# Token rows of k, b and y's scale made by TensorE from channel rows, with a third buffer of channel rows

## The chip, the cores and the metric

The kernel runs on one core of a Trainium2 chip. The metric is the device time of one launch in microseconds (us). Three runs of the kernel before gave 715.59, 718.26 and 719.21 us, a median of 718.26 us. The profiled execution took 721.54 us.

## The reference

Two stages follow one another. The first is a linear recurrence with a 40 x 40 state for each of 4 batches and 8 heads (32 sequences) over 768 steps; the second is a layer norm and a two-layer network on rows of 320 numbers (8 heads x 40).

```
for t in range(S):
    y[:, :, t] = einsum('bhd,bhde->bhe', rt, state)
    Sa = einsum('bhde,bhe->bhd', state, at)
    state = state * wt - Sa x bt + vt x kt
...
xn = (x - mean) / sqrt(var + 1e-06) * g_ln
out = x + maximum(xn @ w_ch1, 0.0) @ w_ch2
```

Everything is fp32. The weights arrive as float64 words and are turned to fp32 pairs in the kernel.

## The kernel before, in words

**Chunks.** The 768 steps are cut into 24 chunks of 32 steps. Within a chunk the recurrence becomes matrix products and a triangular solve, and only the 40 x 40 state passes from chunk to chunk. Running products of the decays w (a scan) scale a, b, k and y so that this works.

**prep(c)** (L137) works on *channel rows*: the tile `et` has 104 partitions (two halves of 40 channels at partitions 0 and 64), and holds w, a, and b and k of 16 sequences each. VectorE scans w forward (gE, L145) and backward (qE, L149), multiplies a by qE into `aT` (L156) and b, k in place by gE (L161); from chunk 6 on GpSimd does the two products. ScalarE copies aT into the block-diagonal `abd` (L160), TensorE multiplies b, k with abd (L174), VectorE applies a sign mask (`gk`, L179), and SyncE's queue writes gk and aT to device memory (d_g L186, d_a L190). `et` has two buffers, so that load_e(c+2) (L135) waits for the matmuls L174 of chunk c.

**load_cl(c)** (L306) does part of it a second time on *token rows* (128 partitions of batch and step): the tile `clt` brings w, k and b in that layout (L309). VectorE checks w (`wild`, L311), scans it both ways (L317, L321, with the reciprocal L320), and transposes both scans in 32 x 32 blocks (L325, L327; the second, `pi`, is y's scale). GpSimd multiplies k and b by the first (eight instructions, L335) into `xk[c % 2]`, and ScalarE copies that into its second half (L340).

**invert / invert2** (L193, L222) invert the triangular matrices of a slab of 2 or 4 chunks on VectorE (L204/L207, L237/L241). **chain(c)** (L361) is the step from state to state: right-hand sides (L368), solve (L348 to L358, or L264 to L275 for the first three slabs), new state (L380, then L386 on VectorE). **state(c)** and **post(c)** (L391, L405) make y: transposes (L397, L412), products (L425, masked in L431), and y (L439) from `xk`, scaled by `pi` into `xt` (L443).

**The network.** moe(g) (L589) handles two chunks. After norm (L553) there are ten blocks f, each with 8 matmuls into `ps_1` (L611), a relu on ScalarE (`hh`, L614), its remainder on VectorE (`hl`, L615), and 6 matmuls that add into two `ps_2` tiles `po` (L597). The result leaves through `ot` (L630). The six buffers of `xt` are freed by that last step.

**Order.** The opening (L661 to L703) is in hand-set order for VectorE and ScalarE; everywhere else a scheduler places instructions on each engine by priority and by its estimate of when an operand is ready. `BOOST` and `NUDGE` (L40, L41) shift priorities: preps have 2000 in their favour, load_cl -300. In L740, 90 groups of two filler matmuls (`warm`, L217) get the lowest priority of all. Each group takes one of the two `ps_2` buffers, and these are handed out in program order: the tiles `po` of the first moe come behind all 90. All DMAs of the loop go through SyncE's one queue, in order.

Of the kernel before, what the change touches and what calls it, by code (L numbers as in the profile page):

```python
# [11 lines left out]
F32 = mybir.dt.float32  # L12
# [22 lines left out]
AHEAD = 4  # L35
EARLY = 6
# [3 lines left out]
BOOST = dict(cg=-300, wg=-600, iv=-600, og=300, pg=2000)  # L40
# [5 lines left out]
def body(ctx, tc, et_in, cl_in, vr, rd, vt, w1, w1x_in, w2, gl, fe, fd, out):  # L46
# [30 lines left out]
    wild = const.tile([128, 10, C], U32, name="wild")  # L77

    et = [stat.tile([128, 2065], F32, name=f"et{i}") for i in range(2)]
# [6 lines left out]
    abd = stat.tile([128, 16, 2, C], F32, name="abd")  # L86
# [9 lines left out]
    def masks():  # L96
        for t, fills in ((sign, (-1.0, 1.0)), (mask, (1.0, 1.0))):
# [25 lines left out]

    d_g = [dr.tile([2, C, 32 * len(s), C], F32, name=f"d_g{i}") for i, s in enumerate(SLABS)]
# [3 lines left out]
    def load_e(c):  # L128
        if c < AHEAD:
            for r0 in HROW:  # L130
                sync.dma_start(out=et[c % 2][r0:r0 + D], in_=et_in[c, r0:r0 + D])
                if c == r0 == 0:
                    sync.dma_start(out=et[0][D:64], in_=et_in[0, D:64])
        else:
            sync.dma_start(out=et[c % 2][0:104], in_=et_in[c])  # L135

    def prep(c):  # L137

        t = et[c % 2]
        n = 528  # L140
        g = pre.tile([128, 16, 33], F32, name="gE")
        q = pre.tile([128, 16, 33], F32, name="qE")
# [8 lines left out]
            initial=0.0, op0=ALU.mult, op1=ALU.max)  # L151
        aT = pre.tile([128, 528], F32, name="aT", bufs=2)
# [5 lines left out]
        for hf in range(2):  # L158
            rs = slice(HROW[hf], HROW[hf] + D)
            nc.scalar.copy(out=abd[rs, :, hf], in_=aT[rs, 0:512].rearrange("p (h t) -> p h t", t=C))  # L160
# [9 lines left out]
        pg = pool_.tile([128, 2, 8, C], F32, name=name)  # L170
        for h in range(8):
            for bb in range(2):
                p = 8 * bb + h
                nc.tensor.matmul(  # L174
                    pg[64 * bb:64 * bb + 64, :, h], lhsT=t[R, 1041 + 64 * p:1105 + 64 * p],
                    rhs=abd[R, p], start=True, stop=True)
# [3 lines left out]
            out=gk, in0=pg.rearrange("p x h t -> p (x h) t"),  # L180
# [3 lines left out]
        for bb in range(2):  # L184
            m = 16 * (2 * k + bb)
            sync.dma_start(  # L186
                out=d_g[si][:, :, m:m + 16].rearrange("x a n t -> (x a) (n t)"),
# [784 lines left out]
```

## Time and profile before

| | before |
|---|---|
| median of 3 runs | 718.26 us |
| profiled execution | 721.54 us, of which 719.7 us are the span from the first to the last instruction |
| TensorE busy (matmul) | 594.4 us, 83% |
| VectorE busy | 579.7 us, 81% |
| ScalarE busy | 327.6 us, 46% |
| GpSimd busy | 287.1 us, 40% |
| mean granted TensorE clock | 0.885 |

Busy time of TensorE includes 73.4 us of filler matmuls (L217). The views read below are the table of groups (for each line: count, busy time, mean duration), the table by stretches of time (busy time of each engine, granted clock, share of the DMA engines), the waits, and single rows of the timeline.

### The profile page before, as it was taken

How to read it: one execution, taken by the hardware profiler on the slowest of the kernel's cores; microseconds unless marked ns; L12 is line 12 of the kernel's file. 1: busy time of each engine (PE TensorE's matmuls, PEld its weight loads, DVE VectorE, ACT ScalarE, POOL GpSimd, SP SyncE). 2: the span in 40 equal slices, each digit the busy share in tenths (PEclk: the TensorE clock that was granted, in tenths of full speed). 3: DMA queues.
4: the chain of work that ended last, by engine and by line, in shares of the span. 5: the costliest groups of instructions: out<-in, count | busy, mean ns of one | idle time of the engine just before them, and what ended most of it. 6: DMA issues, size and time to landing. Idle time of an engine off the chain costs nothing.

```text
span 719.7 us, 24705 instructions
## 1 busy us (share of the span) xinstructions
PE 594.4 (83%) x10386; PEld 525.3 (73%) x10386; DVE 579.7 (81%) x1290; ACT 327.6 (46%) x816; POOL 287.1 (40%) x328
## 2 busy tenths in 40 slices
PE   2786778877668878898878898888989888999995
PEld 2775667766557767787777777777868777889995
DVE  6888797999879949899859999969996989764631
ACT  3324666453333535344354445445536355656221
POOL 8514388456442416254415515623333213333000
PEclk9998878888798979797989988998999999999998
DMA  7787966556562557544567644776346434420100
GB/s 176 193 213 212 291 157 156 150 121 149 125 164 86 127 143 166 126 114 115 110 162 145 144 119 119 146 177 137 97 106 117 108 86 108 105 65 16 41 20 22
DMA packets 155380, 92.35 MB, mean 128 GB/s; under 512 B 126152, under 2 KB 136136, under 8 KB 152840
## 3 DMA queue, kind: packets, MB, share of 16 engines
q1 hardware_dynamic: 155264, 90.72, 52.1%
q8 instruction: 83, 1.36, 0.8%
q14 instruction: 33, 0.27, 0.1%
HBM read 72.06 MB, written 18.64 MB: 126 GB/s over the span
## 4 chain that ended last, share of the span: by engine, by line
DVE 38%; PE 27%; DMA 21%; ACT 6%; issue 5%; SPq 3%; POOL 0%; DVEq 0%; ACTq 0%
DMA et<-in_et_dram 11%; PE ps L611 9%; PE ps L597 8%; DVE yinv L207 5%; DVE ytmp L204 5%; DVE qE L149 3%; DMA r<-in_w_dram 3%; DVE gE L145 3%; DVE x L386 3%; DVE x5s L431 3%; DVE hl L615 2%; DMA d_tt<-yinv 2%; ACT x L358 2%; PE ps L217 2%; PE ps_a L412 1%
## 5 line engine op out<-in xcount | busy, mean ns | idle before, releaser
L611 PE MATMUL ps<-xh,w 128*128 128x256 f32 x480 | 123.5, 315 | 0.9 <-DVE xl L585 0.5
L597 PE MATMUL ps<-w,hh 128*128 128x320 f32 x480 | 118.7, 343 | 3.7 <-DVE ot L630 1.8
L614 ACT ACTIVATE hh<-ps 128x256 fp32r<-128x256 f32 x120 | 45.5, 382 | 129.8 <-PE ps L611 126.1
L611 PEld LDWEIGHTS ps<-xh,w 128*128 128x128 f32 x480 | 92.4, 211 | 5.9 <-issue 2.3
L597 PE MATMUL ps<-w,hl 128*128 128x320 f32 x240 | 77.4, 348 | 18.5 <-DVE hl L615 18.5
L597 PEld LDWEIGHTS ps<-w,hh 128*128 128x128 f32 x480 | 83.1, 206 | 7.8 <-ACT hh L614 2.3
L615 DVE SCALAR_TENSOR_TENSOR hl<-ps,hh 128x256 fp32r<-128x256 f32 x120 | 49.5, 415 | 45.5 <-ACT hh L614 43.0
L161 POOL TENSOR_TENSOR et<-et,gE 104x1024 f32<-104x1024 f32 x18 | 40.4, 2246 | 100.1 <-DVE gE L145 81.7
L217 PE MATMUL ps<-start,ident 128*128 128x160 f32 x360 | 73.4, 362 | 0.0
L611 PE MATMUL ps<-xl,w 128*128 128x256 f32 x240 | 73.3, 305 | 0.0
L204 DVE TENSOR_TENSOR ytmp<-yinv 128x30 f32<-128x30 f32 (+19 forms) x150 | 63.7, 425 | 6.6 <-DMA yinv<-d_g 4.7
L207 DVE TENSOR_TENSOR yinv<-yinv,ytmp 128x30 f32<-128x30 f32 (+19 forms) x150 | 64.4, 429 | 2.2
L217 PEld LDWEIGHTS ps<-start,ident 128*128 128x128 f32 x360 | 63.4, 233 | 2.3
L597 PEld LDWEIGHTS ps<-w,hl 128*128 128x128 f32 x240 | 47.6, 209 | 22.5 <-DVE hl L615 21.5
L145 DVE TENSOR_TENSOR_SCAN gE<-et,start 104x528 f32<-104x528 f32 x24 | 32.3, 1348 | 27.9 <-DMA et<-in_et_dram 27.7
L611 PEld LDWEIGHTS ps<-xl,w 128*128 128x128 f32 x240 | 50.9, 212 | 0.5 <-issue 0.3
L380 PE MATMUL ps_c<-x,xk 104*40 104x40 f32 (+1 forms) x1472 | 45.8, 212 | 3.6 <-ACT x L275 3.0
L160 ACT COPY abd<-aT 40x512 f32<-40x512 f32 x48 | 29.5, 615 | 41.7 <-DVE aT L156 19.1
L439 PE MATMUL ps_a<-xk,x5s 128*32 128x40 f32 (+1 forms) x1536 | 31.9, 213 | 19.0 <-DVE x5s L431 18.8
L386 DVE TENSOR_TENSOR x<-ps_c,x2s 40x320 f32<-40x320 f32 x92 | 44.8, 487 | 2.0
L380 PEld LDWEIGHTS ps_c<-x,xk 104*40 104x40 f32 (+1 forms) x1472 | 37.8, 125 | 11.3 <-ACT x L275 4.3
L358 ACT COPY x<-ps_c 32x160 f32<-32x160 f32 x144 | 40.7, 283 | 9.1 <-PE ps_c L353 6.0
(173 smaller groups left out, 1356.7 us busy)
## 6 DMA issues: line engine op xcount, KB each, us to landing
et<-in_et_dram SPq DMA_DIRECT2D x20, 838.9 KB
clt<-in_cl_dram SPq DMA_DIRECT2D x24, 485.5 KB
d_g<-gk SPq DMA_DIRECT2D x48, 128.0 KB
x<-in_vt_dram SPq DMA_DIRECT2D x48, 128.0 KB
d_a<-aT SPq DMA_DIRECT2D x24, 214.5 KB
vu<-in_vr_dram SPq DMA_DIRECT2D x24, 208.0 KB
x2s<-d_a SPq DMA_DIRECT2D x48, 82.5 KB
x5s<-in_rd_dram SPq DMA_DIRECT2D x48, 80.0 KB
```

Source lines behind the costliest of these rows:

```text
L145: nc.vector.tensor_tensor_scan(out=flat(g[R]), data0=t[R, 0:n], data1=flat(start0[R]), initial=0.0, op0=ALU.mult, op1=ALU.max)
L161: (nc.gpsimd if c >= EARLY else nc.vector).tensor_tensor(out=kb, in0=kb, in1=g[R, :, 0:C].unsqueeze(2).broadcast_to([104, 16, 2, C]), op=A ...
L204: nc.vector.tensor_tensor(out=tv, in0=y[0:n, j + 1:, j:j + 1].broadcast_to([n, m, j]), in1=y[0:n, j:j + 1, 0:j].broadcast_to([n, m, j]), o ...
L207: final["inv", si] = nc.vector.tensor_tensor(out=y[0:n, j + 1:, 0:j], in0=y[0:n, j + 1:, 0:j], in1=tv, op=ALU.add)
L217: nc.tensor.matmul(pw[:, 0:w], lhsT=ident, rhs=start0.rearrange("p h t -> p (h t)")[:, 0:w], start=True, stop=True)
L358: nc.scalar.copy(out=dst[:, :, :, j, 0:D], in_=pu[32 * j:32 * j + 32, :, :, hf])
L380: nc.tensor.matmul(pst[r0:r0 + D, h], lhsT=XK[FROW[hf], 1, hf, p], rhs=X2[FROW[hf], hf, p, 0:D], start=True, stop=True)
L386: nc.vector.tensor_tensor(out=X2n[r0:r0 + D, hf, ps, 0:D], in0=pst[r0:r0 + D], in1=pc.unsqueeze(2).broadcast_to([D, 8, D]), op=ALU.mult)
L597: nc.tensor.matmul(po[u], lhsT=l[:, us], rhs=ws[f"w2_{f}"][:, x], start=f == 0 and n == 0, stop=f == 9 and n == 2)
L611: nc.tensor.matmul(ph, lhsT=l, rhs=r, start=n == 0, stop=n == 7)
L614: nc.scalar.activation(out=hh, in_=ph, func=AF.Relu)
L615: nc.vector.scalar_tensor_tensor(out=hl, in0=ph, scalar=0.0, in1=hh.bitcast(F32), op0=ALU.max, op1=ALU.subtract)
```

## The change

load_cl is gone, and with it the tensor `cl`. The check of w (`wild`) moves into prep on channel rows (16 x 32 columns in place of 10 x 32). A new generator tokens(c) turns the scaled k, b in `et` and the scan qE to token rows: 64 matmuls with the identity matrix into three PSUM tiles, three ScalarE copies into `kt`, and one DMA of kt to a buffer `d_kb` in device memory. load_kb(c) replaces load_cl's end: two DMAs bring k, b into both halves of `xk[c % 2]` (so that GpSimd's products and ScalarE's copies go), and a third brings `pi`. `abd` goes as well: the products L174 become 32 matmuls on halves of 40 rows instead of 16 on 104, and read aT itself. `et` has three buffers (gE and qE two). Since the two halves of d_g change places, sign and indices follow. tokens(c) gets priority 0 ("tg"), load_cl's -300 is dropped; every other number stays.

```diff
-BOOST = dict(cg=-300, wg=-600, iv=-600, og=300, pg=2000)
+BOOST = dict(wg=-600, iv=-600, og=300, pg=2000)
...
-    et = [stat.tile([128, 2065], F32, name=f"et{i}") for i in range(2)]
+    et = [stat.tile([128, 2065], F32, name=f"et{i}") for i in range(ET)]
...
-        for hf in range(2):
-            rs = slice(HROW[hf], HROW[hf] + D)
-            nc.scalar.copy(out=abd[rs, :, hf], in_=aT[rs, 0:512].rearrange("p (h t) -> p h t", t=C))
...
-        for h in range(8):
-            for bb in range(2):
-                p = 8 * bb + h
+        for p in range(16):
+            for hf in range(2):
+                rs = slice(HROW[hf], HROW[hf] + D)
                 nc.tensor.matmul(
-                    pg[64 * bb:64 * bb + 64, :, h], lhsT=t[R, 1041 + 64 * p:1105 + 64 * p],
-                    rhs=abd[R, p], start=True, stop=True)
+                    pg[64 * hf:64 * hf + 64, p], lhsT=t[rs, 1041 + 64 * p:1105 + 64 * p],
+                    rhs=aT[rs, 32 * p:32 * p + 32], start=True, stop=True)
...
+    def tokens(c):
+        t, q = et[c % ET], qs_at[c]
+        pool_, name = (ps_1, "ps_1") if c <= AHEAD else (ps_a, "ps_a")
+        kt = pre.tile([128, 24, D], F32, name="kt")
+        for bb in range(2):
+            px = pool_.tile([128, 8, D], F32, name=name)
+            for h in range(8):
+                for hf in range(2):
+                    p, rs = 8 * bb + h, slice(HROW[hf], HROW[hf] + D)
+                    nc.tensor.matmul(
+                        px[ZROW[hf]:ZROW[hf] + 64, h], lhsT=t[rs, 1041 + 64 * p:1105 + 64 * p],
+                        rhs=ident[rs, rs], start=True, stop=True)
+            nc.scalar.copy(out=kt[:, 8 * bb:8 * bb + 8], in_=px)
+            yield
+        px = pool_.tile([128, 8, D], F32, name=name)
+        for h in range(8):
+            for b in range(4):
+                rs = slice(HROW[b // 2], HROW[b // 2] + D)
+                nc.tensor.matmul(
+                    px[32 * b:32 * b + 32, h], lhsT=q[rs, 8 * (b % 2) + h, 1:33],
+                    rhs=ident[rs, rs], start=True, stop=True)
+        nc.scalar.copy(out=kt[:, 16:24], in_=px)
+        sync.dma_start(out=d_kb[c], in_=kt)
+        yield
...
-    def load_cl(c):
...
+    def load_kb(c):
+        for hf in range(2):
+            rs = slice(ZROW[hf], ZROW[hf] + 64)
+            sync.dma_start(
+                out=xk[c % 2][rs, :, hf].rearrange("p x n e -> p x (n e)"),
+                in_=d_kb[c][rs, 0:16].rearrange("p n e -> p (n e)").unsqueeze(1).broadcast_to([64, 2, 16 * D]))
+        cls[c] = jit.tile([128, 8, D], F32, name="pi", bufs=3)
+        sync.dma_start(out=cls[c], in_=d_kb[c][:, 16:24])
```

The scheduler places nearly everything anew. Three places matter below. The first is TensorE's row where the network's second product (L597, in the changed kernel L601) first appears. Before, it stands in the solve of chunk 3 (L264), between the last filler groups (L217):

```order
L611 MATMUL ps_2737<-xl,w1x 128x256
L412 MATMUL ps_a<-ident,x_1_94 104x32 x8
L217 MATMUL ps_1374<-start_88,ident 128x160 x2
L217 MATMUL ps_1377<-start_88,ident 128x160
L264 MATMUL ps_c<-hbd,tt 32x40 x32
L597 MATMUL ps_2647<-w_0_2208,hh 128x320 x2
L597 MATMUL ps_2647<-w_0_2208,hl 128x320
L597 MATMUL ps_2647<-w_1_2330,hh 128x320 x2
```

In the changed kernel (filler L248, first product L615) the last two filler groups and the first rows of that product read:

```order
L248 MATMUL ps_1872<-start_88,ident 128x160 x2
L248 MATMUL ps_1875<-start_88,ident 128x160 x2
L601 MATMUL ps_3464<-w_0_3010,hh 128x320 x2
L601 MATMUL ps_3464<-w_0_3010,hl 128x320
L601 MATMUL ps_3464<-w_1_3147,hh 128x320 x2
L601 MATMUL ps_3464<-w_1_3147,hl 128x320
```

Counted along TensorE's rows, this place has moved back from the solve of chunk 3 to behind the solve of chunk 10. When chunk 10's right-hand sides are done, 30 blocks of the network's first product stand ahead of them before, 4 in the changed kernel; when chunk 11's are done, 35 in both. At the end of chunk 10's right-hand sides 58 of the 90 filler groups have run in the changed kernel; before, all 90 had by the end of chunk 3's y. At the last chunk's y, 104 of the 120 first products stand ahead before, and 102 in the changed kernel.

The second place is SyncE's queue about chunk 8: before, the loads for y (L300 to L304) and the state, and one load of clt.

```order
L297 DMA x_0_93<-in_vt_dram 32x1024
L304 DMA x5s_98<-in_rd_dram 40x512
L284 DMA x2s_96<-d_a_117 40x528
L285 DMA x2s_96<-d_g_134 32x2x256
L284 DMA x2s_96<-d_a_117 40x528
L285 DMA x2s_96<-d_g_134 32x2x256
L309 DMA clt<-in_cl_dram 128x971
```

In the changed kernel the two loads of xk (L341), the load of pi (L345) and the write of d_kb (L221) stand among the same transfers:

```order
L331 DMA vu<-in_vr_dram 104x16x32
L334 DMA rbd<-in_rd_dram 40x16x32 x2
L230 DMA yinv<-d_g_158 128x32x32
L341 DMA xk_101<-d_kb_137 64x2x640 x2
L335 DMA x5s_99<-in_rd_dram 40x512 x2
L345 DMA pi<-d_kb_138 128x320
L137 DMA et_92<-in_et_dram 104x2065
L221 DMA d_kb_143<-kt 128x960
```

Since d_kb_130 is the buffer of chunk 0, chunk 7's xk is loaded here while chunk 13's kt is already being written: what load_kb reads was written some six chunks earlier.

The third place is VectorE's row. Before, the group of load_cl stands between the rows of the network (L615, L630, L585); here the transpose for one chunk and the scans for the next:

```order
L615 SCALAR_TENSOR_TENSOR hl<-ps_5179,hh 128x256
L325 STREAM_TRANSPOSE gt__5269<-gC 128x10x32
L615 SCALAR_TENSOR_TENSOR hl<-ps_5218,hh 128x256
L630 SCALAR_TENSOR_TENSOR ot<-ps_4387,xt 128x320
L311 SCALAR_TENSOR_TENSOR wild<-clt,wild 128x320
L317 SCALAR_TENSOR_TENSOR gC<-clt,start_88 128x330
L320 RECIPROCAL last<-gC 128x10
L585 TENSOR_TENSOR xl<-ps_5251,xh 128x3x128
L321 SCALAR_TENSOR_TENSOR qC<-clt,last 128x330
```

In the changed kernel only the check is left (L155), behind prep's forward scan (L148); the other rows here are the backward scan of the chunk before (L152), the new state (L390) and the sign mask (L182):

```order
L390 TENSOR_TENSOR x_1_95<-ps_c,x2s_97 40x8x40 x4
L148 SCALAR_TENSOR_TENSOR gE<-et_91,start_88 104x528
L155 SCALAR_TENSOR_TENSOR wild<-et_91,wild 104x512
L152 SCALAR_TENSOR_TENSOR qE<-et_93,last 104x528
L151 RECIPROCAL last<-gE 104x16
L182 TENSOR_TENSOR gk<-ps_a,sign 128x512
```

Six instructions per chunk go from VectorE and one comes back in another shape; prep of one chunk now overlaps with that of the next, as the third et buffer and the second gE and qE buffers allow.

More of the change, by code (lines that the diff above doesn't have):

```diff
@@ L761, in preps, with toks @@
                 yield
+    def toks(first):
+        for c in range(first, NCH):
+            yield from tk[c]
     nth = Counter()
@@ L788, in body @@
             load_v(2)
[L789 to L791 removed]
+            load_kb(2)
         bst("ch", ch[c])
```

126 lines of the change are left out of this document (46 added, 80 removed).

## The prediction

> **What bounds the kernel now.** I read the page first: busy time of the engines, the chain that ended last by engine, and its largest DMA entry.
>
> ```profile
> PE 594.4 (83%) x10386; PEld 525.3 (73%) x10386; DVE 579.7 (81%) x1290; ACT 327.6 (46%) x816; POOL 287.1 (40%) x328
> DMA packets 155380, 92.35 MB, mean 128 GB/s; under 512 B 126152, under 2 KB 136136, under 8 KB 152840
> DVE 38%; PE 27%; DMA 21%; ACT 6%; issue 5%; SPq 3%; POOL 0%; DVEq 0%; ACTq 0%
> ```
>
> No engine is full. VectorE and TensorE are about equally loaded, and the chain changes between them. So I cut the span into stages; the timeline gives the cuts, the ends of chunk 4's, 10's, 11's, 15's and 23's right-hand sides (L368):
>
> ```profile
> 179.80 0.63 PE L368 MATMUL ps_c<-x,x2s 104*32 104x40 f32 x46
> ...
> 352.82 0.34 PE L368 MATMUL ps_c<-x,x2s 96*32 96x40 f32 x12
> 382.40 0.80 PE L368 MATMUL ps_c<-x,x2s 96*32 96x40 f32 x64
> 483.27 0.93 PE L368 MATMUL ps_c<-x,x2s 96*32 96x40 f32 x64
> 652.61 0.80 PE L368 MATMUL ps_c<-x,x2s 96*32 96x40 f32 x64
> ```
>
> Busy time by stage (columns: stretch, length, busy us of the five rows, granted TensorE clock, DMA share, GB/s):
>
> ```profile
> 0.00:180.00 180.00, 129.10 (x2412) 114.97 (x2414) 154.81 (x307) 81.59 (x179) 100.67 (x118) 0.85 0.71 182
> 180.00:353.00 173.00, 142.54 (x2598) 123.44 (x2583) 146.65 (x314) 73.65 (x183) 69.81 (x70) 0.83 0.54 129
> 353.00:383.00 30.00, 23.44 (x450) 20.77 (x441) 21.43 (x44) 12.95 (x35) 10.13 (x10) 0.89 0.61 142
> 383.00:484.00 101.00, 87.71 (x1530) 77.15 (x1517) 90.11 (x194) 48.32 (x125) 47.06 (x49) 0.86 0.62 140
> 484.00:653.00 169.00, 153.31 (x2807) 133.54 (x2807) 142.31 (x371) 89.65 (x238) 55.24 (x77) 0.96 0.45 102
> 653.00:720.00 67.00, 58.24 (x674) 55.44 (x661) 24.35 (x64) 21.44 (x57) 4.20 (x8) 0.96 0.09 23
> ```
>
> VectorE leads until 484 us (154.81, 146.65 and 90.11 us), then TensorE (153.31 of 169, 58.24 of 67).
>
> **What goes.** On VectorE the six instructions of load_cl (the last row is the transpose L325 alone, busy over the whole span):
>
> ```profile
> L317 DVE TENSOR_TENSOR_SCAN gC<-clt,start 128x330 f32<-128x330 f32 x24 | 21.8, 908 | 0.0
> L321 DVE TENSOR_TENSOR_SCAN qC<-clt,last 128x330 f32<-128x330 f32 x24 | 21.2, 884 | 0.2
> L327 DVE STREAM_TRANSPOSE pi<-qC 128x320 f32<-128x320 f32 x24 | 17.9, 747 | 0.0
> L311 DVE SCALAR_TENSOR_TENSOR wild<-clt,wild 128x320 uint32<-128x320 uint32 x24 | 11.8, 493 | 4.9 <-DMA clt<-in_cl_dram 4.9
> L320 DVE RECIPROCAL last<-gC 128x10 f32<-128x10 f32 x24 | 5.0, 209 | 0.2
> 0.00:720.00 720.00, 18.00 (x24) 0.89 0.53 128
> ```
>
> Their mean durations make 0.91 + 0.88 + 0.75 + 0.49 + 0.21 + 0.75 = 3.99 us per chunk, 96 in all. The check comes back with 512 columns; the nearest row of that width is
>
> ```profile
> L179 DVE TENSOR_TENSOR gk<-ps_a,sign 128x512 f32<-128x512 f32 x19 | 13.0, 683 | 5.0 <-PE ps_a L174 5.0
> ```
>
> so 0.69 us, and VectorE is relieved of 3.3 us a chunk. GpSimd loses L335, ScalarE the copies of abd and into xk, 48 each; kt's three copies of 128x320 from PSUM replace them at L270's price:
>
> ```profile
> 0.00:720.00 720.00, 170.64 (x192) 0.89 0.53 128
> L340 ACT COPY xk<-xk 64x640 f32<-64x640 f32 x48 | 34.7, 722 | 5.5 <-POOL xk L335 4.6
> L160 ACT COPY abd<-aT 40x512 f32<-40x512 f32 x48 | 29.5, 615 | 41.7 <-DVE aT L156 19.1 <-PE ps_a L174 14.6 <-PE ps L217 4.6
> L270 ACT COPY hbd<-ps_c 128x320 f32<-128x320 f32 x6 | 2.6, 426 | 16.7 <-PE ps_c L264 16.7
> ```
>
> (the first row is L335 alone, on GpSimd). ScalarE: 72 x 0.43 = 31 against 64 us; it was no bound, so this counts zero. GpSimd counts only through VectorE, whose two-input instructions stretch beside it:
>
> ```profile
> L149 DVE TENSOR_TENSOR_SCAN qE<-et,last x24: 1187/1264/3173, 10.1 to 485.6; 104x528 f32<-104x528 f32 x24
> L207 DVE TENSOR_TENSOR yinv<-yinv,ytmp 128x30 f32<-128x30 f32 (+19 forms) x150 | 64.4, 429 | 2.2
> ```
>
> L149's longest, 3.17 us, is 2.5 times its median. I take an eighth off L207's 64.4 us, and as much for its partner L204, 16 us of VectorE; half of that on the path, **-8 us** (0 to -16). The Trainium skill, "SBUF — State Buffer", "Who interferes with whom", calls the shared port pair an exclusive lock: a VectorE instruction with two SBUF inputs and a GpSimd one that reads SBUF block each other wholly. The 3.17 us agrees; by that rule the gain would lie nearer to -16.
>
> **What TensorE gets.** Rows of nearest shape, at a full clock:
>
> ```profile
> 518.15 1.10 PE L174 MATMUL ps_a<-abd,et 104*64 104x64 f32 x32
> 520.64 1.43 PE L380 MATMUL ps_c<-x,xk 128*40 128x40 f32 x64
> 678.93 0.78 PE L439 MATMUL ps_a<-xk,x5s 128*32 128x40 f32 x62
> 40.11 11.13 PE L217 MATMUL ps<-start,ident 128*128 128x160 f32 x80
> ```
>
> A matmul leaves two records. Scale of y: 32 matmuls of L439's kind, 0.8 us. k and b: 32 of 64 columns out, between L439's 0.8 and 2.2 (L174's 1.10 for 16, doubled); L380 (two column positions, as here) says 1.43. L174 in its new form: the same bounds, less the 1.10 it costs now. Sum 0.8 + 1.43 + 1.43 - 1.1 = 2.6 us a chunk (1.3 to 4.1).
>
> **SyncE.** One load goes, four transfers come. The wait that is new in this queue is load_kb's on the y matmuls that last read xk; x5s and et queue behind it. Before, GpSimd waited there:
>
> ```profile
> POOL xk L335 <- PE ps_a L439: 130.1, 14, 13.6
> DVE gE L145 <- DMA et<-in_et_dram: 13.3, 6, 3.6
> 367.46 5.66 DMA clt<-in_cl_dram
> ```
>
> (the waits of all, those until 180 us, and one piece of the chain). Then came 170.64/24 = 7.1 us of products and 1.4 of copies; now a transfer of at most clt's 5.66 us. d_kb's write precedes its read by six chunks. I count zero, and keep the queue as a rival. The bytes, 0.8 MB more a chunk or a fifth of 92.35 MB, lift a DMA share of 0.54 to some 0.65.
>
> **Stage by stage.** *To chunk 4* (180 us): VectorE loses 5 x 4.0 and gains about 10 preps x 0.69, and the 13.3 us of waits for et shrink with the third buffer: -13 and up to -13; against it, more preps before chunk 0's y. **-15** (0 to -30).
>
> *Chunks 4 to 11* (203 us). Here the order decides: the network waits behind the filler until chunk 10's solve. First the six chunks without it: VectorE's 146.65 us, less 6 x 3.99, plus 6 x 0.69, less the network's share, of which hl is the first row (this stage) and norm's largest instruction the second:
>
> ```profile
> 180.00:353.00 173.00, 10.26 (x25) 0.83 0.54 129
> L577 DVE TENSOR_SCALAR xn<-xt,mv,rs 128x320 f32<-128x320 f32 x24 | 16.0, 668 | 1.0
> 691.19 0.88 PE ps L597 x6
> 692.07 0.94 PE ps L611 x8
> ```
>
> Five norms move out, at least 5 x 0.67 for this instruction and perhaps three times that with the rest: 9. So 146.65 - 23.9 + 4.1 - 10.3 - 9 = 107.5; at the same busy share (0.85) 127 us, 46 less than 173. Then the debt: 31 blocks instead of 5, each 0.88 + 0.94 = 1.82 us when TensorE is full (the chain's last two rows above), 56.4 us; what else TensorE did in 353 to 383, 23.44 - 9.1 = 14.3, and 2.6 of tokens; 32 filler groups at 11.13/20 = 0.56 us each, 18 if none falls into a gap, I take 8. Sum 81.3, at 95% busy 86 us instead of 30. Together 127 + 86 - 203 = **+10** (-10 to +50).
>
> *To chunk 15* (101): VectorE 90.11 - 4 x 3.3 = 77, TensorE 87.71 + 4 x 2.6 = 98 at clock 0.86. With the clock of the next stage (0.96) 88, at 92% busy 96: **-5** (-15 to +9). *To chunk 23* (169): VectorE 142.31 - 8 x 4.0 = 110, TensorE unchanged at 153.31, since the tokens are done; at 97% busy 158: **-11** (-20 to 0). *The tail*: two more blocks (102 against 104 done), **+4**.
>
> 721.5 - 15 + 10 - 5 - 11 + 4 - 8 = 696.5 us for an execution like the profiled one; the median lies 3 us lower: **694 us**. What is late next is TensorE, from the solve of chunk 10 on.
>
> **Rivals.** *A: the debt is not paid back* (slower). If chunks 4 to 10 are not freed by VectorE's lighter load, but keep the 28.8 us each that 173/6 gives, because xk's, tt's and x2s's transfers pass one queue or because each chunk's chain of short steps is that long, then 46 us more: 740. It decides from 4 us a chunk upwards, at 25.1 us. For it: the chain has 21% DMA and TensorE is left without filler work. Against it: chunks 15 to 23 take 169/8 = 21.1 us even with the network.
>
> *B: the clock falls while the network is held.* The clock was 0.83 to 0.86 where TensorE was 82 to 87% busy, and 0.96 at 91%. Without the network TensorE keeps about 105 us (142.54, less 26 blocks of 1.82/0.9, plus 15.6) for 127; at a clock of 0.6 these become 105 x 0.83/0.6 = 145, at 95% 153 us, 26 more than 127: 720. The Trainium skill, "TensorE: Matmul & The Clock Gate", "HAM oscillation", says that idle gaps over some 3.4 us put TensorE back to half its clock; it speaks against this order. The trace shows lower clocks where TensorE has more gaps, not how far it would fall.
>
> *C: TensorE fills better than I grant.* et's loads are 11% of the chain and go from it:
>
> ```profile
> DMA et<-in_et_dram 11%; PE ps L611 9%; PE ps L597 8%; DVE yinv L207 5%; DVE ytmp L204 5%; DVE qE L149 3%; DMA r<-in_w_dram 3%; DVE gE L145 3%; DVE x L386 3%; DVE x5s L431 3%; DVE hl L615 2%; DMA d_tt<-yinv 2%; ACT x L358 2%; PE ps L217 2%; PE ps_a L412 1%
> ```
>
> With the best ends of the opening (-30) and of the two later stages (-15, -20), 721.5 - 30 + 10 - 15 - 20 + 4 - 8 - 3 = 660.
>
> **How the numbers follow.** Forecast (675 to 714) 0.42; A 0.28; B 0.12; C 0.18. A change of 0.5% (3.6 us) is about what a measurement of this kernel can tell from none. Faster: forecast and C, 0.60; the same: B, 0.12; slower: A, 0.28. The range goes from C's 660 to 735, just short of A's end.
>
> **What would show it.** Right: no L597-like row before about 280 us; then over 20 blocks with TensorE over 90% busy; VectorE near 500 us in all, TensorE's busy time at least as long as before; GpSimd near 120; no long waits of gE for et. Wrong: chunks 4 to 10 at over 25 us each with neither VectorE nor TensorE over 80% busy (A), a clock under 0.7 there (B), or a span under 670 us (C).

## The result, and the profile after

The changed kernel takes **934.37 us** (median of 4 runs, 929.78 to 935.70) against 718.74 us before (715.59 to 725.42): 1.297 times as long (95% interval 1.287 to 1.308). The forecast was 694 us and faster. The profiled execution took 935.70 us, its span is 934.0 us.

Busy time and the chain that ended last, from the page of the changed kernel:

```profile
PE 733.5 (79%) x14226; PEld 661.4 (71%) x14226; DVE 487.9 (52%) x1171; ACT 295.3 (32%) x792; POOL 121.0 (13%) x135
DMA packets 168848, 112.36 MB, mean 120 GB/s; under 512 B 127304, under 2 KB 146504, under 8 KB 166280
PE 46%; DMA 19%; DVE 17%; issue 4%; SPq 3%; ACT 3%; POOL 0%; DVEq 0%; ACTq 0%; POOLq 0%
```

VectorE lost 92 us and GpSimd 166 us, as meant. TensorE got 139 us more, and its share of the chain went from 27% to 46%. By stage, cut at the same places as before (ends of the right-hand sides of chunks 4, 10, 11, 15, 23, now L372; columns: stretch, length, busy us of TensorE's matmuls, its weight loads, VectorE, ScalarE and GpSimd, granted TensorE clock, DMA share, GB/s):

```profile
0.00:240.00 240.00, 149.26 (x3746) 136.00 (x3750) 142.74 (x290) 75.19 (x181) 68.67 (x84) 0.60 0.63 162
240.00:430.00 190.00, 140.09 (x3103) 124.28 (x3094) 94.80 (x223) 47.68 (x130) 23.57 (x15) 0.65 0.55 129
430.00:562.00 132.00, 122.84 (x1480) 110.22 (x1472) 47.51 (x122) 29.89 (x81) 8.94 (x11) 0.91 0.31 77
562.00:698.00 136.00, 106.51 (x2172) 95.62 (x2162) 77.37 (x185) 43.89 (x125) 16.09 (x13) 0.81 0.52 125
698.00:867.00 169.00, 157.68 (x3155) 140.89 (x3153) 102.21 (x291) 79.20 (x223) 3.03 (x9) 0.95 0.51 117
867.00:934.00 67.00, 57.16 (x625) 54.38 (x620) 23.26 (x62) 19.48 (x54) 0.71 (x3) 0.95 0.11 27
```

The last two stages are as long as before (169 and 67 us). All of the loss lies ahead of them: 240 us instead of 180, 322 instead of 203 (second and third row), 136 instead of 101. Up to 430 us neither TensorE nor VectorE is full, and the clock is 0.60 and 0.65 instead of 0.85 and 0.83. The network's second product first runs here in the timeline, before and after:

```profile
193.02 0.56 PE L597 MATMUL ps<-w,hh 128*128 128x320 f32 x2
```

```profile
448.31 0.56 PE L601 MATMUL ps<-w,hh 128*128 128x320 f32 x2
```

Five right-hand sides stand ahead of it before (so it comes in chunk 4's solve, not in chunk 3's as I had counted), eleven after. Where an expectation below says that the network starts at "chunk n", n is this count; only the changed kernel's "chunk 10" is the chunk's number.

What TensorE was given, from the table of groups, shapes apart (busy us, mean ns of a record):

```profile
L208 PE MATMUL ps_a<-ident,et 40*64 40x40 f32 x1216 | 61.5, 263 | 26.4 <-ACT kt L211 10.4 <-DVE gk L182 9.8 <-DVE x5s L435 4.2
L177 PE MATMUL ps_a<-aT,et 40*64 40x32 f32 x1216 | 51.8, 250 | 0.1
L217 PE MATMUL ps_a<-ident,qE 40*32 40x40 f32 x1216 | 21.6, 235 | 4.2 <-DVE gk L182 2.2 <-issue 1.1 <-ACT kt L211 0.9
L208 PE MATMUL ps<-ident,et 40*64 40x40 f32 x320 | 16.4, 265 | 2.4 <-DVE gk L182 2.4
L177 PE MATMUL ps<-aT,et 40*64 40x32 f32 x320 | 12.1, 234 | 2.8 <-DVE et L164 2.8
L217 PE MATMUL ps<-ident,qE 40*32 40x40 f32 x320 | 6.8, 240 | 0.0
```

Single rows of the chain (start, us):

```profile
207.78 3.56 PE ps_a L177 x64
...
495.15 1.99 PE ps_a L177 x64
521.88 1.08 PE ps_a L208 x32
```

Tokens (L208, L217) 106.3 us and the product (L177) 63.9 us, in place of 33.9 us for L174 (26.2 + 7.7 in the same table of before): 136.3 us, 5.7 us a chunk. The same 64 records of L177 take 1.99 or 3.56 us, by the clock. VectorE waits for loads of et, where I had forecast no long waits:

```profile
DVE gE L148 <- DMA et<-in_et_dram: 104.6, 22, 9.9
```

The filler groups went late. Here are the records of the filler (four a group) up to the end of chunk 4's right-hand sides, before and after: 88 groups had run, then 22.5.

```profile
0.00:180.00 180.00, 70.92 (x352) 61.52 (x352) 0.85 0.71 182
```

```profile
0.00:240.00 240.00, 22.46 (x90) 19.24 (x90) 0.60 0.63 162
```

So four suspects, called theories 1 to 4 in the expectations: **1** the hold (the filler groups stand ahead of the network until chunk 10), **2** TensorE's price for tokens and product, **3** the clock, **4** buffers and queues (third buffer, SyncE's order, waits for et).

### The profile page after: what moved, and what is told of

It is laid out like the page before. It is cut to its first block, busy times and chain, and to the rows that moved or that the text cites. A ratio compares the mean times of both kernels' runs of the same rounds, so it can differ in the third digit from the quotient of the medians.

```text
span 934.0 us, 32181 instructions
## 1 busy us (share of the span) xinstructions
PE 733.5 (79%) x14226; PEld 661.4 (71%) x14226; DVE 487.9 (52%) x1171; ACT 295.3 (32%) x792; POOL 121.0 (13%) x135
## 4 chain that ended last, share of the span: by engine, by line
PE 46%; DMA 19%; DVE 17%; issue 4%; SPq 3%; ACT 3%; POOL 0%; DVEq 0%; ACTq 0%; POOLq 0%
PE ps L615 11%; PE ps L601 10%; DMA et<-in_et_dram 9%; PE ps L248 5%; PE ps_a L177 3%; PE ps_a L208 3%; DMA yinv<-d_g 3%; DVE ytmp L235 3%; DVE yinv L238 3%; PE ps_a L443 2%; PE ps_a L429 2%; DMA d_kb<-kt 2%; PE ps_c L384 2%; PE ps_c L372 2%; PE ps_a L416 2%
## 5 line engine op out<-in xcount | busy, mean ns | idle before, releaser
L615 PE MATMUL ps<-xh,w 128*128 128x256 f32 x480 | 122.8, 313 | 8.6 <-DVE hl L619 8.6
L601 PE MATMUL ps<-w,hh 128*128 128x320 f32 x480 | 115.7, 338 | 1.6 <-ACT hh L618 0.8
L601 PE MATMUL ps<-w,hl 128*128 128x320 f32 x240 | 75.5, 340 | 33.7 <-DVE hl L619 33.7
L615 PEld LDWEIGHTS ps<-xh,w 128*128 128x128 f32 x480 | 91.4, 209 | 14.5 <-DVE hl L619 8.9
L248 PE MATMUL ps<-start,ident 128*128 128x160 f32 x360 | 75.2, 370 | 12.9 <-POOL ident masks.py:199 12.9
L148 DVE TENSOR_TENSOR_SCAN gE<-et,start 104x528 f32<-104x528 f32 x24 | 30.2, 1257 | 104.6 <-DMA et<-in_et_dram 104.6
L601 PEld LDWEIGHTS ps<-w,hh 128*128 128x128 f32 x480 | 80.9, 202 | 4.7 <-ACT hh L618 1.5
L208 PE MATMUL ps_a<-ident,et 40*64 40x40 f32 x1216 | 61.5, 263 | 26.4 <-ACT kt L211 10.4
L208 PEld LDWEIGHTS ps_a<-ident,et 40*64 40x64 f32 x1216 | 54.4, 173 | 31.9 <-ACT kt L211 10.6
L248 PEld LDWEIGHTS ps<-start,ident 128*128 128x128 f32 x360 | 65.3, 239 | 15.9 <-POOL ident masks.py:199 12.9
L615 PE MATMUL ps<-xl,w 128*128 128x256 f32 x240 | 73.6, 307 | 0.0
L601 PEld LDWEIGHTS ps<-w,hl 128*128 128x128 f32 x240 | 47.1, 205 | 36.6 <-DVE hl L619 36.1
L164 POOL TENSOR_TENSOR et<-et,gE 104x1024 f32<-104x1024 f32 x18 | 45.9, 2551 | 165.4 <-DVE gE L148 154.1
L235 DVE TENSOR_TENSOR ytmp<-yinv 128x30 f32<-128x30 f32 (+19 forms) x150 | 53.8, 359 | 25.7 <-DMA yinv<-d_g 22.0
L390 DVE TENSOR_TENSOR x<-ps_c,x2s 40x320 f32<-40x320 f32 x92 | 44.9, 488 | 26.5 <-PE ps_c L384 24.4
L583 POOL COPY xn<-xn 128x64 f32<-128x64 f32 x24 | 6.6, 274 | 393.7 <-DVE xn L581 345.8
L384 PEld LDWEIGHTS ps_c<-x,xk 104*40 104x40 f32 (+1 forms) x1472 | 41.8, 142 | 17.9 <-ACT x L306 6.8
L421 ACT COPY vu<-ps_a 40x256 f32<-40x256 f32 x96 | 35.2, 367 | 57.2 <-PE ps_a L416 55.5
L152 DVE TENSOR_TENSOR_SCAN qE<-et,last 104x528 f32<-104x528 f32 x24 | 41.7, 1738 | 22.1 <-PE ps L217 14.2
```

The source lines that it names most:

```text
L152: nc.vector.tensor_tensor_scan(out=flat(q[R])[:, ::-1], data0=t[R, n:0:-1], data1=flat(last[R])[:, ::-1], initial=0.0, op0=ALU.mult, op1=A ...
L164: (nc.gpsimd if c >= EARLY else nc.vector).tensor_tensor(out=kb, in0=kb, in1=g[R, :, 0:C].unsqueeze(2).broadcast_to([104, 16, 2, C]), op=A ...
L208: nc.tensor.matmul(px[ZROW[hf]:ZROW[hf] + 64, h], lhsT=t[rs, 1041 + 64 * p:1105 + 64 * p], rhs=ident[rs, rs], start=True, stop=True)
L235: nc.vector.tensor_tensor(out=tv, in0=y[0:n, j + 1:, j:j + 1].broadcast_to([n, m, j]), in1=y[0:n, j:j + 1, 0:j].broadcast_to([n, m, j]), o ...
L248: nc.tensor.matmul(pw[:, 0:w], lhsT=ident, rhs=start0.rearrange("p h t -> p (h t)")[:, 0:w], start=True, stop=True)
L384: nc.tensor.matmul(pst[r0:r0 + D, h], lhsT=XK[FROW[hf], 1, hf, p], rhs=X2[FROW[hf], hf, p, 0:D], start=True, stop=True)
```

## Experiments

In each set the kernel before ran on the same chip, with medians of 722.45 to 724.74 us; a difference between runs of two sets carries these 2 us (some 6 us against the 718.74 us that stand beside the changed kernel). Medians are of 4 runs unless said. The filler count is L740 before and L747 after, `for _ in range(90):`.

### The hold, and fewer fillers

**24 groups in the changed kernel** (90 becomes 24). 

> The changed kernel with 24 filler groups instead of 90, nothing else. In program order the first network product then follows chunk 5's right-hand side, as before the change, and not chunk 10's. Theory 1 (the hold: the fillers own the buffers ps_2, are placed late, and the network's blocks wait for the last of them): the stages from y of chunk 3 to y of chunk 15, which grew by 116 + 35 us, come back for the most part; 770 to 810 us. Theory 2 (TensorE's price: token products and 40-row products make it the bound, 3.8 to 5.7 us per chunk, 91 to 137 us in all): the order hardly matters, 870 to 935 us. Theory 3 (clock: the granted clock was 0.60 up to 277 us because TensorE had neither fillers nor network there): with still fewer fillers the time to y of chunk 3 stays at 270 us or more, clock under 0.7 there.

Measured: 916.76 us (912.47 to 920.13). Only 17.6 us come back, and the clock stays at 0.50 to 0.59 in every 40 us from 40 to 320 us. Theory 2's range was met: the hold is not the main cause. By 240 us 22.5 groups have run, as with 90, and chunk 4's right-hand sides end at 241.5 us instead of 240.4; so this run takes the hold away and leaves the opening as it was. All the same a kernel without it is the better base for what follows.

**200 groups in the kernel before**. 

> The kernel before with 200 filler groups instead of 90, nothing else. In program order the first network product then follows chunk 10's right-hand side, as in the changed kernel; no token product, two buffers. Theory 1 (the hold): the hold alone costs most of what the change lost: 830 to 890 us, the six or seven chunks without the network at under 25 us each and a debt behind them. Theory 2 (TensorE's price): at most the 110 further fillers at 0.56 us, 62 us: under 785 us.

Measured: 817.71 us, 1.129 times (1.122 to 1.136), +93 us. A little under theory 1's numbers and above theory 2's. The hold is as long as the changed kernel's, but 110 more groups come with it, and the filler is busy 157.9 us instead of 73.4: the two aren't separated in these 93 us. The stretches from chunk 4's right-hand sides to chunk 10's and on to chunk 11's:

```profile
182.00:360.00 178.00, 133.12 (x2372) 114.65 (x2373) 128.90 (x251) 58.24 (x141) 66.73 (x62) 0.79 0.51 118
360.00:472.00 112.00, 106.11 (x1063) 96.44 (x1062) 60.56 (x142) 32.44 (x83) 22.60 (x28) 0.96 0.28 65
```

The six chunks without the network take 178 us, where they took 173 with it, though VectorE has 18 us less to do; filler (70.44 us) stands in the network's place. The held work is then paid in full: 112 us instead of 30.

**24 groups in the kernel before**. 

> The kernel before with 24 filler groups instead of 90; the network starts at chunk 4 in program order, one earlier. Theory 1: no hold to take away, within 15 us of the kernel before (705 to 735). Theory 3 (clock): fillers and early network keep the clock at 0.84 in the first 214 us; without 66 of the fillers the clock before chunk 4 falls under 0.7 and the time to y of chunk 3 (173 us) grows by 30 us or more: 745 or more.

Measured: 756.19 us, 1.041 times (1.034 to 1.047). Fewer fillers lose 31 us here, with this clock in the opening (the stretches start at 40, 80, 120 and 160 us):

```profile
40.00:80.00 40.00, 16.12 (x386) 14.45 (x374) 32.80 (x79) 13.88 (x31) 12.62 (x12) 0.63 0.84 235
80.00:120.00 40.00, 21.00 (x543) 17.55 (x541) 35.71 (x67) 21.45 (x55) 23.94 (x26) 0.50 0.59 159
120.00:160.00 40.00, 18.29 (x466) 15.36 (x470) 38.14 (x72) 21.20 (x50) 25.30 (x26) 0.59 0.58 137
160.00:200.00 40.00, 18.92 (x397) 16.14 (x388) 23.70 (x36) 9.08 (x22) 18.17 (x17) 0.59 0.44 103
```

As theory 3 said: in the kernel before, the clock in the opening goes with the early fillers (0.85 to 180 us with them), and they are worth 31 us. The loss lies there: chunk 4's right-hand sides end at 215.8 us instead of 180.4. That leaves some 25 us of the changed kernel's longer opening (240.4 us) to other causes.

### TensorE's work taken out, and added

**Without the token products and their copies**, a zeroed tile written in their place:

```diff
-        kt = pre.tile([128, 24, D], F32, name="kt")
...
-        nc.scalar.copy(out=kt[:, 16:24], in_=px)
+        kt = ktz
...
         sync.dma_start(out=d_kb[c], in_=kt)
```

> The changed kernel without the 64 token matrix products of a chunk and their copies: a zeroed tile is written as token rows, so k, b and the scale of y are left out of the output; third buffer, product on 40 rows, writes and loads of token rows stay. The network then starts at chunk 3 in program order. Theory 2 (and 1, which goes with it here): 660 to 710 us, TensorE's busy time near 610 us. Theory 4 (the third buffer, the preparations run far ahead, and the in-order queue of transfers, with waits for et of 104.6 us): that part stays, the time to y of chunk 3 over 240 us and 780 us or more in all.

Measured: 806.61 us, in theory 4's range and far above theory 2's. But nothing held the 24 writes of zeros back, and all were issued in the first 120 us (24 x 480 KB), so this run is blurred by traffic that the changed kernel doesn't have there. The next one keeps the writes in place.

**Only TensorE's part out**: the three copies read channel rows directly.

```diff
-            px = pool_.tile([128, 8, D], F32, name=name)
...
-            nc.scalar.copy(out=kt[:, 8 * bb:8 * bb + 8], in_=px)
...
+            nc.scalar.copy(out=kt[0:104, 8 * bb:8 * bb + 8], in_=t[0:104, 1041 + 512 * bb:1361 + 512 * bb])
...
+        nc.scalar.copy(out=kt[0:104, 16:24], in_=q[0:104, 0:10, 1:33])
```

> The changed kernel without the 64 token products; three ScalarE copies of the same size read the same channel rows instead, at the same place, and the write of the token rows waits for them as before, so only TensorE's part goes (k, b and the scale of y are wrong numbers in the output). The network starts at chunk 6 in program order. Theory 2 (TensorE's price, some 105 us of busy time): 800 to 835 us. Theory 4 (buffers and queues): the waits of VectorE for et (104.6 us) stay over 70 us and the time stays over 850. Theory 1 alone (the hold, four chunks shorter): 900 to 920.

Measured: 791.33 us, 143 us below the changed kernel, and a little more than theory 2 said; TensorE is busy 623.6 us, 110 less. VectorE's wait for et falls to 53.5 us, so theory 4's mark isn't there. 67 us are left to the kernel before. The network starts after six right-hand sides here, not eleven, so some of the 143 us may be the hold's (17.6 us by the run with 24 groups).

**Only TensorE's part in**, in the kernel before with 24 groups: the loops of L208 and L217, without copies, behind L174. 

> The kernel before with 24 filler groups, plus the 64 token products of a chunk on TensorE right behind its product, into PSUM that nothing reads: no copy, no transfer, two buffers, the path of cl kept, so that TensorE's part of the change is added alone (the output is the reference's). Compared with the kernel before with 24 groups (756.19 us). Theory 2 (TensorE's price): what taking them out of the changed kernel gave, 110 us of busy time and 143 us of time, comes here as a loss: 850 to 905 us. Rival (TensorE is idle for 194 of 755 us there and takes them in its gaps): under 790 us.

Measured: 877.18 us, +121.0 on 756.19. The gaps don't take them. TensorE's busy time, with 24 groups and then with the tokens as well:

```profile
PE 561.6 (74%) x10122; PEld 493.5 (65%) x10122; DVE 587.5 (78%) x1290; ACT 327.8 (43%) x816; POOL 284.4 (38%) x328
```

```profile
PE 672.1 (77%) x13194; PEld 603.3 (69%) x13194; DVE 577.7 (66%) x1290; ACT 327.5 (38%) x816; POOL 276.4 (32%) x328
```

110.5 us of busy time for 121 us of time, with TensorE's share at 74% without and 77% with them. Why an engine with a quarter of its time free can't take them in its gaps isn't shown: the tokens also take tiles of the PSUM pools that other products use, and hold et until they are done, and neither was tested by itself.

**Only the product's new form**, in the kernel before with 24 groups (the diff's product and gk's transfers, abd and its copies gone). 

> The kernel before with 24 filler groups and the product in the changed kernel's form: 32 products on 40 rows that read aT, no abd and not its two copies of 0.615 us; nothing else (output the reference's; the network starts at chunk 4 as with 24 groups alone, 756.19 us). Theory 2: the new form's 24 us of TensorE's busy time are paid, 765 to 790 us. Rival (as I forecast, the copies on the path to the product were worth more than the records): under 750 us.

Measured: 806.37 us, +50.2, more than either expected. With 24 groups the terms nearly close: 756.2 + 50.2 + 121.0 = 927.4, and the whole change has 916.8. If the two add, all the rest of the change, VectorE's and GpSimd's relief among it, comes to -10.6 us.

**The old product twice**, to see whether the records are the price:

```diff
-        for h in range(8):
+        for h in list(range(8)) * 2:
```

> The kernel before with 24 filler groups and its own product (16 on 104 rows by 64 columns of abd) issued twice into the same PSUM tile, so that TensorE has as many records there as in the new form; copies to abd, the layout of d_g and its transfers as before (output the reference's). If the new form's 50.2 us are its records on TensorE: 790 to 815 us. If they come of what else it changes (transfers of d_g in pieces of 1 KB and not 2 KB, the copies gone, low use of TensorE's rows): under 775 us.

Measured: 768.04 us, +11.9. As many records, but a quarter of the price. Busy time of the product (its larger group), then the stretches from 240 to 600 us; first the old product twice, then the new form, last the product with 24 groups alone:

```profile
L174 PE MATMUL ps_a<-abd,et 104*64 104x64 f32 x1216 | 52.1, 262 | 0.8 <-issue 0.7
```

```profile
240.00:400.00 160.00, 130.30 (x2488) 114.60 (x2489) 132.16 (x285) 68.82 (x173) 65.88 (x67) 0.83 0.55 126
400.00:600.00 200.00, 169.77 (x3183) 149.77 (x3182) 167.58 (x380) 91.45 (x240) 73.66 (x84) 0.91 0.57 128
```

```profile
L170 PE MATMUL ps_a<-aT,et 40*64 40x32 f32 x1216 | 47.8, 241 | 0.4 <-DVE x5s L427 0.2 <-issue 0.2
```

```profile
240.00:400.00 160.00, 120.41 (x2145) 103.85 (x2141) 115.45 (x236) 52.73 (x135) 54.20 (x58) 0.72 0.48 110
400.00:600.00 200.00, 169.68 (x2827) 151.15 (x2826) 161.70 (x355) 76.77 (x206) 71.86 (x77) 0.82 0.52 122
```

```profile
L174 PE MATMUL ps_a<-abd,et 104*64 104x64 f32 x608 | 25.4, 246 | 1.9 <-ACT xk L403 1.0 <-ACT abd L160 0.4 <-DVE x5s L431 0.4
```

The product itself is no dearer (with its smaller group 65.6 against 69.0 us), but the clock is 0.72 and 0.82 in place of 0.83 and 0.91, and TensorE's other work, the same in both, is busy 620.7 - 65.6 = 555 us instead of 581.0 - 69.0 = 512. Against the kernel with 24 groups alone (product 33.7 us, other work 528) the new form adds 32 us in the product and 27 in the other work; the old product twice adds 35 in the product and takes 16 from the other work. So what tells the two forms apart lies in the *other* instructions, and goes with the clock. That the 40 rows (of 128) themselves lower the clock fits, but isn't shown: the copies to abd and the layout of d_g differ as well.

**Both with 90 groups.** 

> The kernel before with its 90 filler groups, plus the 64 token products of a chunk into PSUM that nothing reads; the network then starts at chunk 7 in program order in place of 5. Theory 2: the 121 us that they cost with 24 groups, and up to 30 for the two chunks of hold: 840 to 880 us. Theory 1 as the main cause (the hold): under 790, as the hold is two chunks long here and not five.

> The kernel before with its 90 filler groups and the product in the new form on 40 rows; the network starts at chunk 7 in place of 5. Theory 2: 50 us as with 24 groups, and up to 30 for the hold: 770 to 805 us. Rival (with 90 groups the fillers keep the clock up and the form is paid in idle time): under 750 us.

Measured: with the tokens 1.224 times the kernel before (1.210 to 1.238), some 162 us more (from two runs); with the new form 851.41 us (845.81 to 856.54), +127.7, far above the 50.2 and above my bound. With the new form 24 groups are 45 us *better* than 90, where in the kernel before they are 31 us worse. Either addition makes the scheduler place fillers later (seven right-hand sides ahead of the network's second product, not five). With the new form the clock is 0.70 over the first 265 us; I take it that the opening loses its clock and the middle its network. The two can't be added up with 90 groups (127.7 + 162 is more than the whole loss): they share that part.

### The form of the token products

**16 products of 128 columns** in place of 32 of 64, with four copies of 64 rows (the fence shows the loop for one half hf):

```diff
-                        px[ZROW[hf]:ZROW[hf] + 64, h], lhsT=t[rs, 1041 + 64 * p:1105 + 64 * p],
...
+            for j in range(8):
+                nc.tensor.matmul(
+                    px[:, j], lhsT=t[rs, 1041 + 128 * j:1169 + 128 * j], rhs=ident[rs, rs],
+                    start=True, stop=True)
```

> The changed kernel with the token rows of k and b made by 16 products of 40 x 128 columns in place of 32 of 40 x 64, and four copies of 64 rows in place of two of 128; the order of the fillers and of the network stays as in the changed kernel (held to chunk 10). Theory 2 (TensorE's price): half of the 32 products' records go, some 39 of the 77.9 us that TensorE was busy with them, and what they stretched goes with them: 870 to 900 us. Theory 4 (the third buffer and the in-order queues) and theory 1 (the hold): within 15 us of 934.

Measured: 992.25 us, 58 us *slower*. Half the records were busy nearly twice as long:

```profile
L206 PE MATMUL ps_a<-ident,et 40*128 40x40 f32 x608 | 107.2, 344 | 18.9 <-DVE gk L182 13.3
```

(139.9 us with its second group, against 77.9 in all.) Busy time of these products went up by 62 us and the time by 58: here, too, time follows TensorE. Width isn't the only difference: the row halves no longer take turns, and the copies are four.

**The same with nc.tensor.transpose** in place of the matmul with the identity. 

> As the kernel with 16 wide products for k and b, but by TensorE's transpose (its own operation, one record each in the rows of the kernel before) in place of matrix products with the identity (two records each); order and copies the same. If the price goes by records: half of the 139.9 us that the wide products were busy goes, 992 to 910 or 930 us. If it goes by stationary columns loaded, whatever the operation: 975 to 1000 us.

Measured: 891.34 us, 101 us below the wide products, more than halving the records explains; 41.2 us busy instead of 139.9. (The order isn't quite the same: ten right-hand sides ahead, not eleven.)

**Transposes with the row halves in turn** (loop over j outside, hf inside). 

> As the kernel with 16 transposes for k and b, but the two row halves (rows 0 to 39 and 64 to 103) in turn and not eight of one and then eight of the other, with two PSUM tiles held at once. If the halves work side by side: the 41.2 us that TensorE was busy with them fall to 20 to 28, and the time from 891 to 865 to 880 us. If not: 885 to 900 us.

Measured: 874.34 us, but busy time only went from 41.2 to 38.7 us: not the overlap that I expected. The network starts one chunk earlier in this order (nine ahead, not ten); what gives the 17 us stays open.

**The last one with 24 groups.** 

> The changed kernel with the transposes in turn (874.34 us) and 24 filler groups in place of 90. Theory 2 with a small part for the hold, as between the changed kernel and its form with 24 groups (17.6 us): 845 to 865 us. If the hold was the larger part once TensorE is relieved: under 800 us.

Measured: 834.75 us, the best form of the change that was run, 1.156 times the kernel before (1.149 to 1.163). That is 40 us under the same form with 90 groups and under the expected 845 to 865: with less on TensorE, 66 groups fewer are worth more than the 17.6 us that they were in the changed kernel.

### Buffers, queues, clock

**d_a written from GpSimd's queue** from chunk 6 on (`(sync if c < EARLY else nc.gpsimd).dma_start(out=d_a[c], ...)`). 

> The changed kernel with the write of d_a from chunk 6 on issued by GpSimd, which makes its source, in place of SyncE; the order on TensorE stays (held to chunk 10). Theory 4 (the in-order queue: SyncE waits 86.1 us for aT of GpSimd at that write with the next load of et behind it, and VectorE then 104.6 us for et): that wait of SyncE goes, VectorE's wait for et falls under 60 us, 870 to 905 us. Theories 1, 2 and 3: within 10 us of 934.

Measured: 941.14 us (5 runs). SyncE's wait for aT (86.1 us) is gone, VectorE's for et is not:

```profile
DVE gE L148 <- DMA et<-in_et_dram: 109.4, 21, 10.4
```

That queue wait was harmless. SyncE's other waits stay (80.8 us for ot is the largest); none of them was taken out.

**Two buffers of channel rows**, 24 groups (`ET = 2`). 

> The changed kernel with 24 filler groups (916.76 us) and two buffers of channel rows in place of three. Theory 4 (loads and preparations run too far ahead and their transfers and waits in VectorE's order hold the rest up): under 895 us. Theory 2 (TensorE's price is what there is): 905 to 945 us, VectorE waiting longer for et, off the path.

Measured: 878.93 us, 38 us less, in theory 4's range, where theory 2 said no gain. But with two buffers the load of the next chunk stands ahead of tokens(c) in program order, so that the tokens are made from the wrong chunk's rows (TensorE waits 54.4 us for et at L208 there) and no load waits for them. What this shows is that et, held until the last token product has read it, costs up to 38 us (the network also starts one chunk earlier); not that the third buffer does. A third buffer alone in the kernel before wasn't tried.

**Broad products in the preparations**, 24 groups:

```diff
+        for _ in range(12 if c <= 12 else 0):
+            nc.tensor.matmul(
+                pg[:, 0:5], lhsT=ident, rhs=start0.rearrange("p h t -> p (h t)")[:, 0:160],
+                start=True, stop=True)
```

> The changed kernel with 24 filler groups and, in each of the first 13 preparations, 12 filler products (128 x 128 by 160 columns) ahead of the product, so that as many broad products as the fillers had are spread over the first 13 chunks; the network is held to chunk 8. Theory 3 (the clock falls to 0.5 to 0.6 where TensorE has only small products): the clock up to 320 us rises from 0.55 to over 0.75, the time to y of chunk 3 falls by 30 us or more against the kernel with 24 groups, 850 to 890 us in all. Against it (TensorE's own work bounds these chunks): 156 more products of 0.3 to 0.7 us, 935 to 1000 us, clock as before.

Measured: 929.34 us. The clock rises to 0.59 to 0.76 between 160 and 320 us, not over 0.75 throughout, and the time to the fourth chunk's y doesn't fall. The hold is three chunks longer than with 24 groups alone. Theory 3's gain isn't there, and neither side's numbers tell more.

### VectorE's relief alone

**The work of load_cl left out, with nothing in its place** but three transfers, in the kernel before with 90 groups (the output is left unscaled):

```diff
-        t = jit.tile([128, 971], F32, name="clt")
...
+        sync.dma_start(out=cls[c], in_=cl_in[c, :, 0:CH])
...
+                in_=cl_in[c, rs, 331:].unsqueeze(1).broadcast_to([64, 2, 16 * D]))
```

> The kernel before with the second path of channel rows left out on VectorE, GpSimd and ScalarE: what stands in cl is loaded straight to where the scaled k, b and the scale of y would be (four transfers, of the changed kernel's sizes), unscaled, so the output is wrong; TensorE's work, fillers, order (network from chunk 5) and two buffers as before. My forecast's step (chunks 4 to 10 bound by VectorE, 173 us down to 127, with 10 to 20 us in each of the stages beside them): 640 to 680 us. Theory 2 (TensorE bounds these stages too, so VectorE's relief is worth little even for nothing): 700 to 725 us.

Measured: 703.15 us, 0.972 times (0.966 to 0.979). VectorE is busy 110 us less and GpSimd 172 us less, and it brings 20.5 us:

```profile
PE 575.9 (82%) x10386; PEld 514.3 (73%) x10386; DVE 469.9 (67%) x1146; ACT 292.1 (42%) x768; POOL 115.5 (16%) x136
```

TensorE's share stays at 82%, as before. The stretches to chunk 4's right-hand sides and on to chunk 10's:

```profile
0.00:195.00 195.00, 134.97 (x2442) 120.31 (x2443) 140.76 (x284) 77.93 (x178) 69.07 (x87) 0.79 0.74 181
195.00:351.00 156.00, 130.66 (x2575) 115.21 (x2577) 113.48 (x277) 63.05 (x167) 24.39 (x20) 0.88 0.66 150
```

The opening grows by 15 us at a lower clock, and the six chunks shrink from 173 to 156 us. 20.5 us is what VectorE's and GpSimd's relief is worth in the order and with the buffers of the kernel before. No version that computes the reference and beats the kernel before follows from these runs.

## Why the prediction was wrong, point by point

**"VectorE leads until 484 us", and the gains built on it.** The step that failed first. I scaled chunks 4 to 10 with VectorE at a fixed busy share (0.85): 173 us down to 127, and took -15 and -5 in the stages beside and -8 for GpSimd's contention. VectorE's work there came out even lower than forecast, 94.80 us for 107.5, and the stage took 190 us. A busy share of 0.85 was no bound. With the relief alone the stage took 156 us at a share of 0.73 (the rule gives 113.48/0.85 = 134), and with the network held back and filler in its place (200 groups) 178 us at 0.72. Over the whole kernel the relief gives 20.5 us. TensorE stood at 83%, and stays at 82% when VectorE's share falls to 67%.

The -8 us for GpSimd's contention rested on a relief of 16 us in L204 and L207. That came, and larger: 128.1 us of both before, 103.5 in the changed kernel, 109.0 with the relief alone. Part of its reading was wrong: the 3.17 us of L149 overlap GpSimd's L161, which stays in the changed kernel, and L149 took 1.73 to 1.80 us in four places where it overlapped L335 alone. What the relief was worth on the path can't be told apart from the rest of the 20.5 us.

**"2.6 us a chunk (1.3 to 4.1)" for tokens and product.** At a full clock the rows give 1.99 for L177 and 2 x 1.08 for k and b, where I had put 1.43 each by L380's row; with 0.8 and -1.10 that is 3.85, inside the range. The upper bound (L174's row doubled) was the right row: the same stationary columns and as many records. At the clocks that were granted it was 5.7. And here lies the second step that failed, the dearer one: the stages to chunk 10 have no term for it (2.6 us stand only once in chunk 11 and four times to chunk 15), as if it were hidden there without a reason given. It cost 121.0 + 50.2 us when added alone, more than its own busy time (136.3 us in the changed kernel).

**The clock.** Rival B had it fall only while the network is held (0.12, 720 us). Its rows didn't bear it out: the same table has 0.85 at 72% busy and 0.89 at 78%, and 0.83 at 82%. The clock fell from chunk 1 on: 0.60 over the first 240 us. There the forecast was -15, the result +60. The fillers went late (22.5 groups by then), I take it since the scheduler saw TensorE occupied; that the opening's clock goes with them I had not seen (31 us by the kernel before with 24 groups).

**"The debt": 81.3 us of held work.** The hold came as read from the order (first L601 at 448 us), and in the kernel before a hold as long cost 93 us, its 110 more groups included. Here its removal gave 17.6.

**Rival A** ("chunks 4 to 10 are not freed", 740 us) had the right sign, and its mark was seen: 190/6 = 31.7 us a chunk with TensorE at 74% and VectorE at 50%. Which of my reasons holds for it isn't shown. Of SyncE's queue only d_a's write was tested, and moving it changed nothing; the chain of short steps wasn't tested by itself. That TensorE's tokens alone, with no new transfer, cost 121.0 us speaks against the queue as the main one. B's mark, a clock under 0.7, was seen in the same stage. The range ended at 735 because I priced each rival by itself: TensorE's price, a low clock and a longer hold came together wherever TensorE got more work with 90 groups (the new form alone: 127.7 us).

**"No long waits of gE for et"**: 104.6 us. The third buffer didn't help: et is now held until the token products have read it, and without them on TensorE the wait is 53.5 us (27.7 in the kernel before).

**What held**: VectorE 487.9 ("near 500"), GpSimd 121.0 ("near 120"), "TensorE's busy time at least as long as before", the debt paid with TensorE over 90% busy (122.84 of 132 us), and the two last stages within 11 us. These signs came true in a kernel that is 1.3 times as long: they were signs of the order and of what goes, not of the time.

## What to carry to other kernels

Work moved from an engine that is 81% busy to one that is 83% busy is not hidden because neither is full: add it alone to the old kernel, and take the relief alone, before both are built. Here that would have read +171 (with 24 groups) against -20 (with 90). Price small matrix products by records and stationary columns at the clock of their stage, at half clock too, and ask what a scheduler does with low-priority filler once it believes the engine busy.

## What the runs showed of the hardware

A busy TensorE did not always keep its clock. In the changed kernel, with small products nearly all the time, over half of it in those on 40 rows (L177, L208, L217):

```profile
200.00:240.00 40.00, 35.30 (x940) 32.82 (x934) 17.38 (x30) 10.07 (x27) 7.58 (x5) 0.50 0.61 154
```

88% busy and a clock of 0.50. The Trainium skill, "TensorE: Matmul & The Clock Gate", "Part 1: The HAM clock gate (the "warmup" mystery)", says that the clock is either whole or half and follows how busy TensorE has been of late; the two durations of L177 (1.99 and 3.56 us) agree with the first, this row does not with the second, if busy means what the profile counts.

Products with 40 rows and 128 stationary columns from one row half after the other cost 139.9/768 = 0.18 us a record; with 64 columns and the halves in turn 77.9/1536 = 0.05. Which of the two differences counts isn't separated, and all of these are at mixed clocks. A transpose of 40 x 128 cost 41.2/384 = 0.11 us, and needs one record where the product needs two.
